# Two local attention steps interleaved on TensorE, Silu in place of Tanh behind the attention, and every mask as a matrix product

## The chip, the cores and the metric

The kernel runs on one core of one Trainium2 chip. The metric is the device time of one execution in microseconds (us). Names of engines in the rows: PE is TensorE's matrix products, PEld its weight loads, DVE is VectorE, ACT is ScalarE, POOL is GpSimd, SP is SyncE, which issues most of the DMAs.

## What is computed

Attention over 4 sequences of 576 tokens with 8 heads of 64, as the sum of a pooled global attention and a banded local one, and behind it two feed-forward layers over all 2304 tokens:

```python
out_d = sm_attn(q_d, k_d, v_d)                 # q, k, v averaged over 4 tokens
out_up = np.repeat(out_d, factor, axis=2)
mask = np.abs(pos[:, None] - pos[None, :]) < factor
scores = scale * np.matmul(q, k.transpose(0, 1, 3, 2))
scores = np.where(mask, scores, -1000000000.0)
attn = np.exp(scores - np.max(scores, axis=-1, keepdims=True))
attn = attn / (np.sum(attn, axis=-1, keepdims=True) + 1e-09)
out_local = np.matmul(attn, v)
x = out_up + out_local                         # then (tokens, 512)

g = x @ w_gate                                 # first layer, width 1536
silu = g * (1.0 / (1.0 + np.exp(-g)))
x = silu * (x @ w_val) @ w_out
h = np.maximum(x @ w_in, 0.0)                  # second layer, width 2048
x = h * h @ w_out2
```

## The kernel before

The whole program is generated by a planner. Work is cut into tasks, each a row of stages; a stage has an engine (`t` TensorE, `v` VectorE, `a` ScalarE, `d` a DMA issued by SyncE, `p` one issued by GpSimd), a planned cost in us, buffers that it takes and gives back, and a condition. `Order.run` keeps a clock for each engine and always issues the stage that can start first, so the order of the instructions on every engine follows from planned costs, due times and buffer counts. The chip then runs these fixed streams with semaphores.

Three kinds of work matter here. **Local steps** (`local_task`): a batch has ten blocks of up to 58 queries against a window of 64 keys, and six steps work on them: steps 0, 1, 3 and 4 on two blocks each, step 2 on one block in each half of the sequence. A step of two blocks makes 16 products `scores` of 64x64 (head pairs `hp`, and `h2` for the two heads of a pair, which lie in rows 0 to 63 and 64 to 127); the softmax over 512 elements a partition; `trans`, four transposes of 128x128; and 16 products `pv`, again 64 rows by 64 columns. In both, `h2` or `r` selects rows `64*r` to `64*r+63` of the operands and the same 64 partitions of the result. All are fp32 products, and each leaves two passes (two rows MATMUL and two LDWEIGHTS) in the records, so a step of two blocks has 32 passes of `scores` and 32 of `pv`. For batches 0 and 1 (`MASK_PE` is 2) the mask is laid into the bank first by bf16 products with an identity; for batches 2 and 3 VectorE multiplies and adds it in `masked`. In the first three steps of batch 0 (`early`) the buffers are borrowed from another pool.

**Global tasks** (`global_tasks`, `global_task`) do the pooled attention with products of 72x144 and 72x72. **Units** (`unit_tasks`) do the first feed-forward layer on 256 tokens: twelve products for the gate and twelve for the value into the banks `gv`, an activation, and twelve products down into `y`. The gate is silu as (tanh(g/2) + 1) * g * v / 2: ScalarE's Tanh (`tanh`), and two VectorE operations (`silu`, `times`). The units of a 256-token tile start once its attention is there, so units and attention alternate on TensorE. Behind the attention a second form of the first layer (`b2_unit`, its `tail` the same gate) and the second layer follow.

Local steps take from shared pools: four PSUM banks `att`, five tiles `p`, two tiles `pt` (transposed probabilities) and two tiles `vw` (the values, loaded by SyncE). Where the planner sees TensorE wait for a bank for more than 0.6 us in the first 100 us, `bank` fills 80% of that wait with products of zeros (line L81); in the first 40 us `warm_bank` does the like (L1251).

Of the kernel before, what the change touches and what calls it, by code (L numbers as in the profile page):

```python
# [1 line left out]

# [61 lines left out]
def attn_moe_kernel(ctx: ExitStack, tc: tile.TileContext, qT, kT, vw, vin, vp, qp, kp, qs, ks, vs, maskc, masks, identc, wB, wC, out):  # L64
# [33 lines left out]
    def dma(size):  # L98
        return size / RATE
# [7 lines left out]
    CUT_T, CUT_J, W_LAG, Q_LATE, Q_LATER, MASK_PE = 2, 4, 65.0, 10.0, 6.0, 2  # L107
# [506 lines left out]
    def local_task(b, i, ins, due, bls=(0, 1), early=False):  # L614
# [11 lines left out]
        nb, b0 = len(bls), bls[0]  # L626
# [8 lines left out]
        def scores():  # L635
            half = int(t00 >= S // 2)
            q, k, o = q_t[b, half], k_t[b, half], HALF0[half]
# [7 lines left out]
            for c, (_, _, q0, w0) in enumerate(blocks):  # L645
                for hp in range(HP):
                    for h2 in range(2):
                        r = slice(64 * h2, 64 * h2 + 64)
                        nc.tensor.matmul(  # L649
                            u["s"][r, c * HP + hp],  # L650
                            q[r, hp, q0 - o : q0 - o + WIN],
                            k[r, hp, w0 - o : w0 - o + WIN],
                            start=not mask_pe,
                            stop=not mask_pe or c * HP + hp == n - 1,
                        )
# [14 lines left out]
        def values():  # L670
            v = room(10, 8 * D) if last else att.tile([128, 8 * D], F32, tag="vw", bufs=N_V, name="vw")
            if b < NB:
                u["v"] = v.rearrange("p (a h l d) -> p l a h d", a=2, h=2, d=D)
                nc.sync.dma_start(out=v, in_=vw[b * NPAIR + i].rearrange("p a h l d -> p (a h l d)"))
                return
            u["v"] = v.rearrange("p (l h a d) -> p l a h d", h=2, a=2, d=D)
            heads = vs[b - NB].rearrange("p f -> (p f)").rearrange("(r h t d) -> r t h d", r=2, h=4, d=D)
            for r in range(2):
                for bl, (_, _, _, w0) in zip(bls, blocks):
                    o = v[64 * r : 64 * r + 64].rearrange("p (l h d) -> p l h d", l=2, d=D)[:, bl]  # L680
                    nc.sync.dma_start(out=o, in_=heads[r, w0 : w0 + WIN])
# [14 lines left out]
        def pv():  # L696
            for t in tiles:
                x_tile(t)
            ps = u["ps"] = bank("att")
            pt = u["pt"].rearrange("p (b a h k) -> p b a h k", b=nb, a=2, h=2)  # L700
            for c, (t0, t1, q0, _) in enumerate(blocks):
                for hpp in range(2):
                    for h2 in range(2):
                        for r in range(2):
                            rr = slice(64 * r, 64 * r + 64)
                            o = (2 * h2 + hpp) * 128 + t0 - t00
                            nc.tensor.matmul(  # L707
                                ps[rr, o : o + t1 - t0],
                                u["v"][rr, bls[c], hpp, h2, :],
                                pt[rr, c, hpp, h2, t0 - q0 : t1 - q0],  # L710
                                start=True,
                                stop=True,
                            )
# [19 lines left out]
        tiles = range(x_of(b * S + t00), x_of(b * S + t11 - 1) + 1)  # L733

        def g_need():
            return [t for c in range(t00 * 2 // S, (t11 - 1) * 2 // S + 1) for t in g_tasks[b, c]]

        def ready():
            when, room = after([v_in] + g_need()), x_room(tiles)
            return None if when is None or room is None else max(when, room)  # L740

        def turn():

            return 0.0 if early or all(t.at > len(t.stages) - 4 for t in g_need()) else None

        v_take = () if last else ("v",)
        v_in = Task([Stage("d", dma(128 * 512) * (1 if b < NB else 2), values, v_take, cond=lambda: task.ready)], due)
        if mask_pe:
            cost, share = 0.737 * nb, 0.74
            softmax = softmax_stages(u, n, 128, WIN, "s", float(D) ** -0.5, 1, False, ("att",))  # L750
        else:
# [1692 lines left out]
```

## Time and profile before

| what | value |
|---|---|
| median of 3 runs | 943.49 us (941.63 to 943.52) |
| the profiled execution | 944.18 us |
| its span, first to last instruction | 942.4 us |
| PE busy | 931.2 us, 99% of the span |
| DVE busy | 757.3 us, 80% |
| ACT busy | 584.5 us, 62% |

A busy PE covers the time in which any product is under way, pipelined ones too, so 99% says that TensorE was hardly ever without work, not that each of its products ran at the array's pace. The chain of waits is followed from end to end: a row of it for several products gives the time by which they moved the end on.

### The profile page before, as it was taken

How to read it: one execution, taken by the hardware profiler on the slowest of the kernel's cores; microseconds unless marked ns; L12 is line 12 of the kernel's file. 1: busy time of each engine (PE TensorE's matmuls, PEld its weight loads, DVE VectorE, ACT ScalarE, POOL GpSimd, SP SyncE). 2: the span in 40 equal slices, each digit the busy share in tenths (PEclk: the TensorE clock that was granted, in tenths of full speed). 3: DMA queues.
4: the chain of work that ended last, by engine and by line, in shares of the span. 5: the costliest groups of instructions: out<-in, count | busy, mean ns of one | idle time of the engine just before them, and what ended most of it. 6: DMA issues, size and time to landing. Idle time of an engine off the chain costs nothing.

```text
span 942.4 us, 22566 instructions
## 1 busy us (share of the span) xinstructions
PE 931.2 (99%) x8929; PEld 907.0 (96%) x8929; DVE 757.3 (80%) x1875; ACT 584.5 (62%) x1368; POOL 23.8 (3%) x31
## 2 busy tenths in 40 slices
PE   8999999999999999999999999999999999999997
PEld 6888999999999999999999999999999999999997
DVE  6998969878978878788796999978777666776865
ACT  3878667657667888456542675757565645555553
POOL 0102102000000000000000000000000000000000
PEclk9999999999999999999999999999999999999999
DMA  9998969586678857166553638624315864516131
GB/s 278 262 286 225 243 186 239 179 270 183 225 269 312 265 172 252 50 220 204 187 185 101 211 138 312 244 81 180 126 77 178 316 230 171 180 67 247 47 133 68
DMA packets 101205, 183.82 MB, mean 195 GB/s; under 512 B 22380, under 2 KB 60012, under 8 KB 101100
## 3 DMA queue, kind: packets, MB, share of 16 engines
q1 hardware_dynamic: 97644, 174.42, 54.8%
q0 software_dynamic: 3456, 7.96, 4.8%
q8 instruction: 70, 1.15, 0.5%
q14 instruction: 35, 0.29, 0.1%
HBM read 120.75 MB, written 61.60 MB: 193 GB/s over the span
## 4 chain that ended last, share of the span: by engine, by line
PE 92%; DVE 2%; ACT 2%; DMA 2%; SPq 1%; issue 0%; DVEq 0%
PE gv L1045 11%; PE gv L1047 10%; PE gv L1046 10%; PE y L1045 8%; PE y L1046 8%; PE y L1047 8%; PE att L1983 6%; PE att L1982 6%; PE att L1981 6%; PE att L1046 3%; PE att L1047 3%; PE att L1045 3%; PE att L707 2%; PE att L797 2%; PE att L649 1%; PE y L1251 1%
## 5 line engine op out<-in xcount | busy, mean ns | idle before, releaser
L1045 PE MATMUL gv<-xs,wg 128*128 128x256 f32 x880 | 250.4, 285 | 0.1
L1046 PE MATMUL gv<-xs,wg 128*128 128x256 f32 x880 | 246.9, 281 | 0.0
L1047 PE MATMUL gv<-xs,wg 128*128 128x256 f32 x880 | 246.9, 281 | 0.0
L1045 PEld LDWEIGHTS gv<-xs,wg 128*128 128x128 f32 x880 | 166.2, 189 | 2.1 <-issue 0.4
L1046 PEld LDWEIGHTS gv<-xs,wg 128*128 128x128 f32 x880 | 166.1, 189 | 0.0
L1047 PEld LDWEIGHTS gv<-xs,wg 128*128 128x128 f32 x880 | 166.0, 189 | 0.0
L2132 ACT ACTIVATE f<-rr 128x256 fp32r<-128x256 f32 (+2 forms) x200 | 88.1, 467 | 62.9 <-PE att L1983 25.7
L1983 PE MATMUL att<-wg,f 128*128 128x256 f32 x432 | 122.5, 284 | 0.5 <-DVE f L2135 0.4
L1982 PE MATMUL att<-wg,f 128*128 128x256 f32 x432 | 122.0, 282 | 0.0
L1981 PE MATMUL att<-wg,f 128*128 128x256 f32 x432 | 121.7, 282 | 0.3 <-ACT f L2132 0.3
L2135 DVE TENSOR_TENSOR f<-rr,f 128x512 fp32r<-128x512 f32 (+2 forms) x200 | 94.0, 488 | 27.2 <-ACT f L2132 26.5
L2056 ACT ACTIVATE rr<-rr 128x512 f32<-128x512 f32 (+1 forms) x144 | 80.2, 557 | 31.4 <-DVE rr L2059 29.2
L1045 PE MATMUL y<-xs,wg 128*128 128x256 f32 x336 | 94.6, 281 | 1.1 <-ACT ys L1228 1.1
L1046 PE MATMUL y<-xs,wg 128*128 128x256 f32 x336 | 94.5, 281 | 0.0
L1047 PE MATMUL y<-xs,wg 128*128 128x256 f32 x336 | 94.4, 281 | 0.0
L1981 PEld LDWEIGHTS att<-wg,f 128*128 128x128 f32 x432 | 81.8, 189 | 0.7 <-ACT f L2132 0.7
L1983 PEld LDWEIGHTS att<-wg,f 128*128 128x128 f32 x432 | 81.2, 188 | 1.4 <-DVE f L2135 1.3
L1982 PEld LDWEIGHTS att<-wg,f 128*128 128x128 f32 x432 | 81.5, 189 | 0.0
L2141 DVE TENSOR_TENSOR rr<-rr 128x256 f32<-128x256 f32 (+1 forms) x160 | 62.3, 393 | 7.0 <-ACT rr L2056 4.7
L1045 PEld LDWEIGHTS y<-xs,wg 128*128 128x128 f32 x336 | 63.6, 189 | 1.4 <-ACT ys L1228 1.3
L1047 PEld LDWEIGHTS y<-xs,wg 128*128 128x128 f32 x336 | 63.5, 189 | 0.0
L1046 PEld LDWEIGHTS y<-xs,wg 128*128 128x128 f32 x336 | 63.5, 189 | 0.1
(149 smaller groups left out, 2317.2 us busy)
## 6 DMA issues: line engine op xcount, KB each, us to landing
wst<-wB SPq DMA_DIRECT2D x36, 512.0 KB, 4.9
w_sp<-tmp SPq DMA_DIRECT2D x36, 512.0 KB, 3.8
wg<-w_sp SPq DMA_DIRECT2D x36, 512.0 KB, 5.1
wst<-wC SPq DMA_DIRECT2D x32, 512.0 KB, 5.0
y_sp<-ys SPq DMA_DIRECT2D x29, 512.0 KB, 4.5
xf_sp<-xs SPq DMA_DIRECT2D x24, 512.0 KB, 2.7
xs<-xf_sp SPq DMA_DIRECT2D x24, 512.0 KB, 5.4
ys<-y_sp SPq DMA_DIRECT2D x20, 512.0 KB, 6.7
```

Of the source, the lines that this page charges most:

```text
L707: nc.tensor.matmul(ps[rr, o : o + t1 - t0], u["v"][rr, bls[c], hpp, h2, :], pt[rr, c, hpp, h2, t0 - q0 : t1 - q0], start=True, stop=True,)
L797: nc.tensor.matmul(us[h2]["s"][:, ci], q, kd_t[b][r, hp, :], start=start, stop=stop)
L1045: nc.tensor.matmul(o, w[:, 0], x[:, 0], start=start, stop=False, skip_group_check=more)
L1046: nc.tensor.matmul(o, w[:, 0], x[:, 1], start=False, stop=False, skip_group_check=more)
L1047: nc.tensor.matmul(o, w[:, 1], x[:, 0], start=False, stop=stop, skip_group_check=more)
L1981: nc.tensor.matmul(o, h, w[:, 0], start=first and not again and c == 0, stop=False, skip_group_check=again)
L1982: nc.tensor.matmul(o, h, w[:, 1], start=False, stop=False, skip_group_check=again)
L1983: nc.tensor.matmul(o, l, w[:, 0], start=False, stop=end, skip_group_check=again)
L2056: return lambda: nc.scalar.activation(out=whole(f, c0), in_=whole(f, c0), func=func)
L2132: nc.scalar.activation(out=fac(k, 0), in_=source(), func=AF.Copy)
L2135: nc.vector.tensor_tensor(out=fac(k, 1), in0=source(), in1=fac(k, 0).bitcast(F32), op=ALU.subtract)
L2141: go = lambda: nc.vector.tensor_tensor(out=o(), in0=a(), in1=b(), op=op)
```

## The change

The stage functions of `local_task` go into `local_lane`, and `local_task` now takes one or two lanes. With two lanes the products of `scores` alternate between them, and so do those of `pv`. Lane 1 exchanges the two halves of the result: products from rows `h2` write partitions of `h2 ^ lane`, into a bank of its own, so that lane 0 uses the two tiles of the array on its diagonal (rows 0, columns 0 and rows 1, columns 1) and lane 1 the two others. Its values are loaded with the halves exchanged. In batch 0 steps 3 and 4 form a pair and the other four stay alone; in batches 1 to 3 the pairs are 0 and 1, the two halves of 2, and 3 and 4. A pair takes two banks `att` for `scores`, two tiles `pt`, both tiles `vw` and two banks for `pv` together; its softmax and transposes stay per lane. `MASK_PE` becomes 4. Units whose activation is planned once all attention is done use ScalarE's Silu and one VectorE product, and `tail` always does.

```diff
-    CUT_T, CUT_J, W_LAG, Q_LATE, Q_LATER, MASK_PE = 2, 4, 65.0, 10.0, 6.0, 2
+    CUT_T, CUT_J, W_LAG, Q_LATE, Q_LATER, MASK_PE = 2, 4, 65.0, 10.0, 6.0, 4
...
+        def score(at):
+            half = int(t00 >= S // 2)
+            q, k, o = q_t[b, half], k_t[b, half], HALF0[half]
+            c, hp = at // HP, at % HP
+            _, _, q0, w0 = blocks[c]
+            for h2 in range(2):
+                nc.tensor.matmul(
+                    u["s"][rows(h2 ^ lane), c * HP + (hp ^ lane)],
+                    q[rows(h2), hp, q0 - o : q0 - o + WIN],
+                    k[rows(h2), hp, w0 - o : w0 - o + WIN],
...
-                nc.sync.dma_start(out=v, in_=vw[b * NPAIR + i].rearrange("p a h l d -> p (a h l d)"))
+                whole = vw[b * NPAIR + i].rearrange("p a h l d -> p (a h l d)")
+                if lane:
+                    for r in range(2):
+                        nc.sync.dma_start(out=v[rows(r)], in_=whole[rows(1 - r)])
+                else:
+                    nc.sync.dma_start(out=v, in_=whole)
...
+        def value(at):
+            pt = u["pt"].rearrange("p (b a h k) -> p b a h k", b=nb, a=2, h=2)
+            c, hpp, h2 = at // 4, at // 2 % 2, at % 2
+            t0, t1, q0, _ = blocks[c]
+            for r in range(2):
+                o = (2 * h2 + hpp) * 128 + t0 - t00
+                nc.tensor.matmul(
+                    u["ps"][rows(r ^ lane), o : o + t1 - t0],
+                    u["v"][rows(r), bls[c], hpp, h2, :],
+                    pt[rows(r), c, hpp, h2 ^ lane, t0 - q0 : t1 - q0],
...
+    def local_task(b, parts, ins, due, early=False):
+
+        lanes = [local_lane(b, i, bls, lane, early) for lane, (i, bls) in enumerate(parts)]
...
+        def scores():
+            for x in lanes:
+                x.masks()
+            for at in range(n):
+                for x in lanes:
+                    x.score(at)
+
+        def pv():
+            for x in lanes:
+                x.begin()
+            for at in range(4 * nb):
+                for x in lanes:
+                    x.value(at)
...
+        cost = 0.63 * nb + nl * 0.107 * nb * (b < MASK_PE)
+        p_take, pt_take, pt_give, v_take = ("p",) * nl, ("pt",), ("pt",) * nl, ("v",)
...
-        halves = ((0, (0, 1)), (1, (0, 1)), (2, (0,))), ((2, (1,)), (3, (0, 1)), (4, (0, 1)))
+        both = (0, 1)
+        ends_ = [(3, both), (4, both)]
+        if b < NB:
+            lanes = [[(0, both)], [(1, both)], [(2, (0,))]], [[(2, (1,))], ends_]
+        else:
+            lanes = [[(0, both), (1, both)]], [[(2, (0,)), (2, (1,))], ends_]
...
         def tanh():
             u["s"] = com.tile([128, T1], F32, tag="sg", bufs=N_SG, name="sg")
+            u["half"] = 0.5 if turned_all() is None else 1.0
+            if u["half"] == 1.0:
+                nc.scalar.activation(out=u["s"], in_=u["g"][:, :n], func=AF.Silu)
+                mid.stages[0].give = mid.stages.pop(1).give
+                return
             nc.scalar.activation(out=u["s"], in_=u["g"][:, :n], func=AF.Tanh, scale=0.5)
...
-            def tanh():
+            def silu():
                 room(t)
-                nc.scalar.activation(out=u[t], in_=gate(), func=AF.Tanh, scale=0.5)
-
-            def silu():
-                nc.vector.scalar_tensor_tensor(out=u[t], in0=u[t], scalar=1.0, in1=gate(), op0=ALU.add, op1=ALU.mult)
+                nc.scalar.activation(out=u[t], in_=gate(), func=AF.Silu)
 
             def times():
-                nc.vector.scalar_tensor_tensor(out=u[t], in0=u[t], scalar=0.5, in1=val(), op0=ALU.mult, op1=ALU.mult)
+                nc.vector.tensor_tensor(out=u[t], in0=u[t], in1=val(), op=ALU.mult)
```

On TensorE, before, the first two local steps of batch 2 stand behind the last products of the global attention (`vd`), one step after the other, each with its own bank:

```order
L1047 MATMUL gv_2416<-xs_1864,wg_1382 128x256
L835 MATMUL att_2445<-pt_2413,vd_1250 64x72 x4
L835 MATMUL att_2452<-pt_2429,vd_1250 64x72 x4
L649 MATMUL att_2462<-kT_1139,qT_1178 64x64 x16
L649 MATMUL att_2490<-kT_1139,qT_1178 64x64 x16
L1045 MATMUL y_2034<-hh_2405,wg_1347 128x256
```

In the changed program the same two steps are one stage, which begins with three mask products (two of 256 columns for the first lane, one of 512 for the second), and the two banks alternate, two products each; the last two rows repeat seven times more:

```order
L881 MATMUL att_2591<-pt_2585,vd_1260 64x72 x4
L649 LDWEIGHTS ident_b_82
L649 MATMUL att_2599<-mask_b_81,ident_b_82 128x256
L649 LDWEIGHTS ident_b_82
L649 MATMUL att_2599<-mask_b_81,ident_b_82 128x256
L649 LDWEIGHTS ident_b_82
L649 MATMUL att_2602<-mask_b_81,ident_b_82 128x512
L657 MATMUL att_2599<-kT_1128,qT_1192 64x64 x2
L657 MATMUL att_2602<-kT_1128,qT_1192 64x64 x2
```

So the sixteen products of bank `att_2602`, which stood behind those of the other bank, now stand between them. Over the whole program the 64x64 products (`scores` and `pv`) lie in 39 unbroken stretches before and in 24 now, mask products go from 16 (12 of 256 columns, 4 of 512) to 32 (24 and 8), and the products of zeros that `bank` puts in from 28 to 49.

On VectorE, behind the attention, a unit's gate before takes L1089 (`silu`) when ScalarE's Tanh is done and L1094 (`times`) when the value is:

```order
L1103 TENSOR_TENSOR hh_5628<-sg_5586,hh_5628 128x256
L379 SCALAR_TENSOR_TENSOR wf_5662<-wst_5434,bits_75 128x512
L1089 SCALAR_TENSOR_TENSOR sg_5660<-sg_5660,gv_5632 128x256
L1366 TENSOR_TENSOR wf_5681<-wf_5606,wf_5662 128x256
L1366 TENSOR_TENSOR wf_5662<-wf_5662 128x256
L1094 SCALAR_TENSOR_TENSOR sg_5660<-sg_5660,gv_5665 128x256
```

After the change only `times` (now L1153) is left of the two:

```order
L1153 SCALAR_TENSOR_TENSOR sg_5319<-sg_5319,gv_5343 128x256
L1418 TENSOR_TENSOR tmp_5358<-wf_5142,tmp_5358 128x512
L1418 TENSOR_TENSOR wg_5363<-wf_5356,wg_5363 128x512
L1162 TENSOR_TENSOR hh_5381<-sg_5319,hh_5381 128x256
L1153 SCALAR_TENSOR_TENSOR sg_5336<-sg_5336,gv_5365 128x256
```

Here the gate's bank is free as soon as ScalarE has read it. That happens in 18 units and in all 54 tails, so 72 VectorE operations leave; ScalarE gains one load of an activation table, ahead of its first Silu.

## Rows read from the trace of the kernel before

**Rows 1.** The page, part 1: busy us (share of the span) xinstructions.

```profile
PE 931.2 (99%) x8929; PEld 907.0 (96%) x8929; DVE 757.3 (80%) x1875; ACT 584.5 (62%) x1368; POOL 23.8 (3%) x31
```

**Rows 2.** Busy time of each engine in stretches (us from the span's start).

```profile
core 0: us, PE busy (x) PEld busy (x) DVE busy (x) ACT busy (x) POOL busy (x), PEclk, DMA share, GB/s
0.00:40.00 40.00, 35.79 (x457) 30.01 (x459) 30.87 (x76) 21.89 (x59) 4.71 (x9) 1.00 0.92 258
40.00:100.00 60.00, 59.76 (x803) 53.16 (x804) 55.62 (x154) 49.10 (x142) 9.52 (x11) 1.00 0.92 264
100.00:270.00 170.00, 169.72 (x2089) 160.51 (x2088) 141.45 (x369) 108.53 (x283) 9.54 (x11) 1.00 0.74 217
270.00:360.00 90.00, 88.92 (x757) 88.62 (x755) 74.59 (x161) 75.61 (x152) 0.00 (x0) 1.00 0.76 255
```

**Rows 3.** Who waited for whom, TensorE: total us, times, longest us.

```profile
PE y L1251 <- ACT zeros L1245: 2.4, 1, 2.4
PE att L649 <- DMA qT<-qT: 1.3, 1, 1.3
PE y L1045 <- ACT ys L1228: 1.1, 1, 1.1
```

**Rows 4.** The chain in order of time, 64x64 stretches: start us, us, what.

```profile
51.04 1.08 PE att L649 x32
...
59.27 1.07 PE att L707 x32
...
185.64 1.54 PE att L707 x48
...
227.60 0.11 PE gv L1047
227.71 2.01 PE att L649 x64
229.72 0.31 PE gv L1045
230.04 0.12 PE gv L1046
```

**Rows 5.** The chain, global attention's products and the transposes.

```profile
57.27 0.59 PE att L686 x4
...
80.33 0.40 PE att L835 x8
...
125.26 1.14 PE att L797 x16
...
140.26 0.64 PE att L797 x8
...
142.76 0.65 PE att L835 x16
```

**Rows 6.** The chain, transposes of two and products of zeros.

```profile
18.97 0.87 PE y L1251 x8
...
54.52 0.37 PE att L686 x2
```

**Rows 7.** Groups by line: busy us, mean ns of one, idle before, releaser.

```profile
L649 PE MATMUL att<-kT,qT 64*64 64x64 f32 x640 | 23.2, 221 | 1.3 <-DMA qT<-qT 1.3
```

**Rows 8.** Groups by line and shape, VectorE and ScalarE.

```profile
L1089 DVE SCALAR_TENSOR_TENSOR sg<-sg,gv 128x256 f32<-128x256 f32 x54 | 22.4, 415 | 6.0 <-ACT sg L1081 5.5
...
L1798 DVE SCALAR_TENSOR_TENSOR ss<-ss,gv 128x256 f32<-128x256 f32 x30 | 12.5, 415 | 8.2 <-ACT ss L1795 8.1
...
L661 DVE SCALAR_TENSOR_TENSOR p<-att,mask 128x256 f32<-128x256 f32 x12 | 4.5, 405 | 0.0
L661 DVE SCALAR_TENSOR_TENSOR p<-att,mask 128x512 f32<-128x512 f32 x4 | 2.7, 674 | 0.0
```

**Rows 9.** Groups of ScalarE in the first 8 us.

```profile
L1245 ACT ACT_TABLE_LOAD x1 | 1.3, 1283 | 0.7 <-PEq L2434 0.7
```

**Rows 10.** The chain: a load of values that landed late.

```profile
95.21 9.48 DMA vw<-vs
```

More of the change, by code (lines that the diff above doesn't have):

```diff
@@ L644, in scores @@
                 nc.tensor.matmul(u["s"][:, c0:c1], ident_b, m, start=c0 == 0, stop=False)
[L645 to L655, printed above, removed]
+        def score(at):
[8 more added lines that the diff above has]
+                    k[rows(h2), hp, w0 - o : w0 - o + WIN],
+                    start=not mask_pe,
+                    stop=not mask_pe or at == n - 1,
+                )
         def masked():
@@ L773, in local_task @@
-        for t in tiles:
-            x_parts[t].append(task)
-        return task
+            if before and not early and not before.done:
+                return None
+            return 0.0 if early or all(t.at > len(t.stages) - 4 for t in g_need) else None
+        cost = 0.63 * nb + nl * 0.107 * nb * (b < MASK_PE)
+        p_take, pt_take, pt_give, v_take = ("p",) * nl, ("pt",), ("pt",) * nl, ("v",)
+        if early:
+            p_take, pt_take = ("xs",) * 3 * lanes[0].first, ()
+            pt_give = ()
+            if lanes[0].last:
+                pt_give = tuple(lambda k=k: ("xs", early_room[k][0]) for k in range(3))
+                v_take = ()
@@ new lines, in local_task @@
+        v_in = [Task([Stage("d", x.load, x.values, v_take, cond=lambda: head.ready)], due) for x in lanes]
+        head = Task([Stage("t", cost, scores, ("att",) * nl + p_take, (), lambda: after(ins + [consts]), 0.7)], due)
+        mids = []
+        for x in lanes:
+            x.softmax[0].cond = lambda: after([head])
+            mids.append(
+                Task(
+                    x.softmax
+                    + [
+                        Stage("t", 0.22 * nb, x.trans, ("att",) + pt_take, () if early else ("p",), turn, 0.98),
+                        Stage("a", act(n * WIN, True), x.turned, (), ("att",)),
+                    ],
+                    due,
+                )
+            )
@@ L777, in global_tasks @@
+        val = Task([Stage("t", 0.64 * nb, pv, ("att",) * nl, pt_give + v_take * nl, ready, 0.7)], due)
+        ends = [Task([Stage("v", dve(232 * nb), x.to_x, (), ("att",), lambda: after([val]))], due) for x in lanes]
+        head.then = [*v_in, *mids, val, *ends]
+        if not early:
+            val_before[0] = val
+        for x, end in zip(lanes, ends):
+            for t in x.tiles:
+                x_parts[t].append(end)
+            att_ends[b].append(end)
+        return head
     def global_tasks(b, ins, due, combos, end=False):
@@ L869, in global_task @@
         return task
-    att_tasks = {}
+    att_tasks, att_heads, att_ends = {}, {}, {b: [] for b in range(B)}
     def x_due(token):
```

93 lines of the change are left out of this document (35 added, 58 removed).

## The prediction, made before the changed kernel ran

> **What bounds the kernel now.** I read the busy times first: TensorE works in 99% of the span, VectorE in 80%, ScalarE in 62% [rows 1]. A high share alone can mislead, so next came who waits. TensorE's waits are few and short: 2.4 us for its first operand, 1.3 us for the first queries, and 1.1 us for ScalarE's copy out of `y` near 358 us [rows 3]. The attention therefore runs at TensorE's pace, and what shortens TensorE's list shortens the kernel, as long as the others keep up. The stretches say where that is tight: from 40 to 100 us VectorE is busy 55.62 of 60 us, from 100 to 270 us 141.45 of 170 [rows 2]. Batch 0 and most of batch 1 fall in the first of these.
>
> **What a local step costs TensorE.** In the chain a stretch of 32 passes of `scores` takes 1.08 us and one of 64 takes 2.01 [rows 4]. The 32 more cost 0.93, so a pass costs 29.1 ns, and 1.08 - 32 x 0.0291 = 0.15 us is paid once for each stretch. For `pv`, 48 passes against 32 give (1.54 - 1.07) / 16 = 29.4 ns. After a stretch the first product of a unit moves the end by 0.31 us where a product usually moves it by 0.12 [rows 4]: up to 0.19 more. A stretch therefore costs 0.15 to 0.34 us beyond its passes.
>
> **Do four tiles run at once?** Before, a 64x64 pass and its partner use the two diagonal tiles, a round of two in 58 ns. No row has four tiles at work, so I bound it by what pairs show. The pace of one tile alone is that of the fp32 transposes: two passes more, of 128 columns each, take 0.59 - 0.37 us [rows 5, 6], 0.11 us a pass or 0.86 ns a column. By it 144 columns take 0.124 us; L797, whose two products lie in different row halves and the same columns, takes (1.14 - 0.64) / 8 = 0.0625 us a pass [rows 5], half of that. And 72 columns take 0.062 us; L835, whose products share rows and lie in different column halves, takes (0.65 - 0.40) / 8 = 0.031 [rows 5], half again. Sharing rows costs nothing and sharing columns costs nothing, so I take it that four passes need the 58 ns of two. That is one end; the other is 117 ns, two rounds. The first is nearer to the rows, since each pair among the four tiles is of a kind that overlaps fully there.
>
> A rule speaks against it. Rows show that the two row halves of `scores` write into one bank in the same round: 640 passes keep TensorE busy for 23.2 us [rows 7], where one after another they would take 640 x 58 ns = 37 us. The Trainium skill, page "TensorEngine Tiling (Array Packing)", section "Restrictions and Gotchas", says that different row tiles cannot access the same PSUM bank simultaneously. By that rule `scores` could not run as it does; if it held, two passes for each bank would follow each other and the gain below would be gone. The measurement decides: it doesn't hold for halves of a bank, and the gain stays.
>
> **The sum, against the profiled execution (944.18 us, 0.7 above the median of the runs).**
>
> 1. Paired passes. Batches 1 to 3 have ten paired blocks each, batch 0 four: 34 blocks x 16 passes = 544 of `scores` and as many of `pv`. 1088 x 29.2 ns = 31.8 us; four at a time they take half: **-15.9 us** (between that and 0). Nothing hides them, since TensorE is the engine that is waited for.
> 2. Stretches. 39 become 24: 15 x 0.25 us, the middle of the two prices above, **-3.8 us** (-2.3 to -5.1).
> 3. Masks. 16 more products, twelve of 256 columns and four of 512, are 20 times 256 columns. Eight products of zeros of that width take 0.87 us [rows 6], 0.109 each: **+2.2 us** on TensorE. VectorE loses the sixteen operations of L661, 4.5 + 2.7 = 7.2 us [rows 8], and then reads its maximum and difference out of PSUM, as it does now for batches 0 and 1.
> 4. Products of zeros. 21 more x 0.109 = **+2.3 us**. They stand for 80% of waits for banks, because a pair takes two of four; the rest of these waits is **+0.6 us**. The low end is 0 for both, if these waits coincide with others.
> 5. VectorE before 100 us. With 4.4 us to spare in 60 [rows 2], it can't follow all of the gain there. Roughly a third of the paired passes fall before 100 us, 5 us of the gain; I take **+1.0 us**, from 0 to 5.
> 6. Silu. 72 VectorE operations of 0.415 us leave [rows 8], 30 us, all behind the attention, where TensorE doesn't wait for VectorE; a gate is ready some 0.4 us sooner. I cost it at **0**: TensorE's other units cover the gate before and after. At most it takes away the 1.1 us wait near 358 us [rows 3]. The table load takes 1.28 us on ScalarE [rows 9], once; queued behind it are that unit's own gate and copies for weights, with units ready on TensorE, and from 270 to 360 us ScalarE has 14 of 90 us to spare [rows 2]. Without that cover it would cost 1.3 us. Silu itself isn't in the trace; I price it as Tanh, which it replaces one for one.
> 7. Values. A pair holds both `vw` tiles, so the next loads wait until its `pv` is done. The slowest load took 9.48 us [rows 10], and between one `pv` and the next the new order has ten us of other products or more. I cost it at **0**, up to 4 us if some land late. What waits behind such a `pv` is all of TensorE's queue. Transposes likewise wait for both `pt` tiles, again behind units that are ready.
>
> Sum: -15.9 - 3.8 + 2.2 + 2.3 + 0.6 + 1.0 = -13.6, so 930.6 us on the profiled execution's own time and some 929.9 against the median. **I predict 930 us.**
>
> **Rivals.**
>
> *TensorE is limited by issue, not by the array.* A `pv` pass has 58 moving columns, a `scores` pass 64, yet both take 29 ns [rows 4]: columns alone don't set the round. If it is the rate at which passes and weight loads are issued, four take twice as long as two, and terms 2 to 5 without the VectorE part remain: 944.18 - 3.8 + 2.2 + 2.3 + 0.6 = 945.5, no change. For it: that equality. Against it: weight loads, which are 64 columns wide in both, explain it as well, and they are per tile. Chance 8%. Halfway between the two ends, a round of 88 ns, half of term 1 is left: 937.5 us, 5%. The Trainium skill, page "TensorE: Matmul & The Clock Gate", section "Wait — 56ns, not 53.3ns?", says that start-to-start never drops below about 25 ns a matmul. No stretch here has a mean below 29, so the trace can't refute it; by that figure a round would take 100 ns and the kernel, an estimate, some 941 us.
>
> *The planned order stalls.* VectorE can't follow before 100 us (5 us of term 5 lost) and some values land late (4 us of term 7): 939 us. For it: VectorE's 93% there, and both `vw` tiles taken. Against: the same engine ran at 93% before and TensorE waited for it nowhere long. 12%.
>
> *Slower: tiles that share rows or columns drain between lanes.* The interleaving puts an off-diagonal pair behind each diagonal one. If each change of pair pays what a stretch pays once, 0.15 us in place of 0.058 [rows 4], 544 changes cost 544 x 0.092 = 50 us, some 995 us; at a fifth of that price 955. It decides as soon as a round of four exceeds 117 ns by 2 or 3. Against it: L797 and L835 overlap partners that share columns or rows. 6% for any price; 2% more for other losses above 16 us.
>
> **How the numbers follow.** My forecast has 67%, stalls 12%, half of the overlap 5%, issue 8%, drain and other losses 8%. Its own range is 926 to 934: the low end takes the higher price of a stretch and no cost for zeros (-1.3 - 2.9), the high end the larger part of the costs of terms 5 and 7. Over all cases 926 to 942 holds about 80%: it reaches over the stalls and the half overlap and leaves out issue and drain. 0.2%, 1.9 us, is about what a measurement of this kernel can tell from no change. Faster by more: 67 + 12 + 5 = 84%; within it, 8% (issue); slower, 8%.
>
> **What would show it.** In the changed kernel's chain a stretch of 64 passes should take about 1.1 us, like 32 now; 2.0 means no overlap, 1.55 half of it. The mask rows of L661 and 72 of VectorE's products should be gone without a change in TensorE's waits; ScalarE should show a second table load after 250 us with no TensorE wait beside it. TensorE waiting for loads of `vw`, for VectorE before 100 us, or for ScalarE near 345 us would show terms 5 to 7 wrong. TensorE's busy sum should fall by some 14 us; if it falls and the span doesn't, the stalls have taken it. The prediction is wrong if four tiles don't overlap.

## The result and the profile after

The changed kernel takes 933.64 us, the median of 4 runs (932.06 to 934.34); the kernel before took 943.5 beside it (941.63 to 943.8). The ratio is 0.9897 with a 95% interval of 0.9879 to 0.9915, so it is faster by 1.0%. The prediction was 930 us with a range of 926 to 942. The profiled execution of the changed kernel took 932.06 us, the fastest of its runs, against 944.18 before: 12.1 us less.

Line numbers have moved: `scores` is L657 now, `pv` L720, the mask products L649, the zeros L82, a unit's three kinds of products L1099 to L1101, the join of a weight tile L380.

The first part of the page answers to [rows 1]: TensorE's busy sum fell by 14.4 us, VectorE's by 28.6.

```profile
PE 916.8 (99%) x8966; PEld 893.5 (96%) x8966; DVE 728.7 (78%) x1787; ACT 585.7 (63%) x1369; POOL 23.7 (3%) x31
```

The stretches of [rows 2] again. From 40 to 100 us TensorE is no longer always busy; from 270 to 360 us VectorE has 7.4 us less to do.

```profile
40.00:100.00 60.00, 58.33 (x884) 52.13 (x881) 55.04 (x153) 47.27 (x137) 9.10 (x11) 1.00 0.99 275
...
270.00:360.00 90.00, 88.73 (x748) 88.04 (x746) 67.20 (x143) 72.13 (x144) 0.00 (x0) 1.00 0.73 242
```

Who waited for whom on TensorE, as in [rows 3]. The first and third rows have their like before. New are waits for VectorE and ScalarE at L1100 and L1099 (both for `h`, the squared gate of a `b2_unit`), and one at L720 for "issue", that is, for nothing that the profile shows. No row names `vw`.

```profile
PE y L1310 <- ACT zeros L1304: 2.4, 1, 2.4
PE att L1100 <- DVE h L1864: 1.2, 1, 1.2
PE y L1099 <- ACT ys L1287: 1.2, 1, 1.2
PE att L720 <- issue: 1.0, 1, 1.0
PE att L1099 <- ACT h L1861: 0.8, 1, 0.8
```

The chain in order of time (start, us, what). A stretch of 64 passes takes 1.09 us, where [rows 4] have 2.01. At 98.69 the one wait for issue stands, behind 127 passes in a row; at 235.82 another 64 of `pv` follow 64 of `scores` directly, without a wait.

```profile
96.68 1.09 PE att L657 x64
97.77 0.92 PE att L720 x63
98.69 1.00 issue
99.70 0.21 PE att L720
...
234.73 1.09 PE att L657 x64
235.82 0.94 PE att L720 x64
```

The groups of [rows 7] and [rows 9]: the passes of `scores` keep TensorE busy for 14.1 us, 23.2 before, and a second table load stands with the first Silu.

```profile
L657 PE MATMUL att<-kT,qT 64*64 64x64 f32 x640 | 14.1, 222 | 0.7 <-DMA qT<-qT 0.7
```

```profile
L1137 ACT ACT_TABLE_LOAD x1 | 1.3, 1283 | 0.0
```

**Where the time came from and went.** I divided TensorE's list at three places and took from each part what its unit products need at the pace they keep wherever nothing disturbs them, 0.118 us from start to start. The attention's part is the start of the last `pv` pass less 0.118 for each unit product ahead of it. The rest of a part is what it loses: behind the attention up to the first product of a `b2_unit` into `y`; from there to the first product of the second layer (the `b2_unit`s); and from there to the last product. All the kernels of this study are in the table, with their median and, as a measure of how far weights are, the number of weight tiles joined (L379 before, L380 after) when TensorE starts its 2050th unit product, early in the `b2_unit`s.

```
kernel                median   attention  lost up   lost in      lost in       weight tiles at
                      us       us         to b2     b2_units     layer 2       product 2050
before                943.5    127.3      0.9       1.2          6.8           50
after                 933.64   112.6      1.1       4.7          5.8           47
e1_lanes_apart        942.85   123.4      0.5       4.7          5.7           47
e2_tanh               938.53   113.0      1.7       9.1          6.7           46
e3_masks_vector       937.30   112.5      2.9       9.2          5.7           46
e4_no_zeros           931.71   115.0      2.1       1.2          5.7           48
e5_before_silu        943.16   127.0      2.7       0.3          5.7           50
e6_before_masks       948.57   130.7      3.7       1.7          6.7           49
e7_dues_19_5          935.98   112.7      3.3       4.0          5.8           47
e9_pairs_alone        939.54   112.4     -0.1      12.4          6.8           45
e10_low_on_gpsimd     940.71   117.9      0.6       9.5          5.7           47
e11_first_3           936.97   113.9      3.1       2.6          9.9           48 (four fewer wanted)
e12_before_first_3    965.15   126.9      2.6       9.3         18.6           48 (four fewer wanted)
e14_no_zeros_early    938.78   117.7      6.1       0.4          5.8           49
```

From before to after the attention gave 14.8 us and the second layer 1.0; the `b2_unit`s took 3.5 back, and 0.1 went behind the attention: 12.1 us. The 3.5 are the loss that no term of the prediction held. Of them 2.7 are TensorE's starts at 368.94 and 376.21 to 376.67, which come 1.41, 0.94 and 0.34 us later than the pace. The wait for `ys` is a matter of where it is counted: its start at 346.69 us, 1.35 late, falls into the `b2_unit`s, and its like before, at 359.15 and 1.25 late, into the column ahead of them. In that column of the changed kernel stand two new late starts instead, by 0.42 us at 268.97 and by 0.31 at 272.49.

The chain there, of the changed kernel: the sums and the gate of a `b2_unit`, whose steps stand between other work on VectorE and ScalarE.

```profile
365.84 0.42 DVE ss L1804
366.33 0.20 issue
366.52 0.40 DVE ss L1857
366.93 0.54 issue
367.46 0.42 DVE ss L1804
367.94 0.18 issue
368.13 0.42 DVE ss L1804
368.55 0.34 DVE h L1864
368.94 0.38 PE att L1100
```

### The profile page after: what moved, and what is told of

It reads as the page before. It is cut to its first block, busy times and chain, and to the rows that moved or that the text cites. A ratio compares the mean times of both kernels' runs of the same rounds, so it can differ in the third digit from the quotient of the medians.

```text
span 930.3 us, 22554 instructions
## 1 busy us (share of the span) xinstructions
PE 916.8 (99%) x8966; PEld 893.5 (96%) x8966; DVE 728.7 (78%) x1787; ACT 585.7 (63%) x1369; POOL 23.7 (3%) x31
## 4 chain that ended last, share of the span: by engine, by line
PE 95%; DVE 2%; ACT 1%; DMA 1%; issue 1%; SPq 0%; DVEq 0%; ACTq 0%
PE gv L1099 11%; PE gv L1101 11%; PE gv L1100 11%; PE y L1099 9%; PE y L1100 8%; PE y L1101 8%; PE att L2038 6%; PE att L2037 6%; PE att L2036 6%; PE att L1100 3%; PE att L1101 3%; PE att L1099 3%; PE att L843 2%; PE att L657 1%; PE att L881 1%; PE att L720 1%
## 5 line engine op out<-in xcount | busy, mean ns | idle before, releaser
L1099 PE MATMUL gv<-xs,wg 128*128 128x256 f32 x880 | 250.4, 285 | 0.3 <-ACT sg L1137 0.3
L1101 PE MATMUL gv<-xs,wg 128*128 128x256 f32 x880 | 246.9, 281 | 0.1
L1100 PE MATMUL gv<-xs,wg 128*128 128x256 f32 x880 | 246.9, 281 | 0.0
L1099 PEld LDWEIGHTS gv<-xs,wg 128*128 128x128 f32 x880 | 166.1, 189 | 2.8 <-issue 1.0
L1101 PEld LDWEIGHTS gv<-xs,wg 128*128 128x128 f32 x880 | 165.9, 189 | 0.3 <-DVE wg L427 0.3
L1100 PEld LDWEIGHTS gv<-xs,wg 128*128 128x128 f32 x880 | 166.0, 189 | 0.0
L1100 PE MATMUL y<-xs,wg 128*128 128x256 f32 x336 | 94.5, 281 | 0.0
L1099 PE MATMUL y<-xs,wg 128*128 128x256 f32 x336 | 94.5, 281 | 0.0
L1101 PE MATMUL y<-xs,wg 128*128 128x256 f32 x336 | 94.4, 281 | 0.0
L1099 PEld LDWEIGHTS y<-xs,wg 128*128 128x128 f32 x336 | 63.5, 189 | 0.2 <-ACT ys L1287 0.2
L1100 PEld LDWEIGHTS y<-xs,wg 128*128 128x128 f32 x336 | 63.5, 189 | 0.1
L1101 PEld LDWEIGHTS y<-xs,wg 128*128 128x128 f32 x336 | 63.6, 189 | 0.0
```

The costliest lines, as they stand in the source:

```text
L1099: nc.tensor.matmul(o, w[:, 0], x[:, 0], start=start, stop=False, skip_group_check=more)
L1100: nc.tensor.matmul(o, w[:, 0], x[:, 1], start=False, stop=False, skip_group_check=more)
L1101: nc.tensor.matmul(o, w[:, 1], x[:, 0], start=False, stop=stop, skip_group_check=more)
```

## The theory and its rivals

Weights reach the chip packed. A tile `wst` costs ScalarE two or three passes (L368, L377, for most also L373) and VectorE the join (L380); then each half of a product's operand is made, one operation on ScalarE (L1414) and one on VectorE (L1418), and for the later weights VectorE forms sums of tiles too (L1425). The queue of weights is worked off beside the attention and the units, in one order, and the `b2_unit`s need weights that come after four groups which only the second layer wants. My theory: the shorter attention takes from ScalarE and VectorE the time in which they unpacked. Product 2050 starts at 370.7 us before and at 357.3 after; from the attention's end to the first `b2_unit` the kernel before joined 18 tiles in 90.2 us, 5 us a tile, so 13.4 us less is 2.7 tiles, and 47 are done in place of 50. This is an estimate of what the planner could place, and the agreement is rough: when the attention ends 31 tiles are joined, 30 before, so all three are lost behind it, and VectorE is not full there (busy for 69.3 of the 93.1 us up to product 2050, 85.6 of 101.7 before). The rows of VectorE's join from the start to that product, of the kernel before and of the changed one:

```profile
L379 DVE SCALAR_TENSOR_TENSOR wf<-wst,bits 128x512 int32<-128x512 int32 x50 | 34.2, 685 | 3.0 <-ACT wst L376 2.5
```

```profile
L380 DVE SCALAR_TENSOR_TENSOR wf<-wst,bits 128x512 int32<-128x512 int32 x47 | 32.3, 688 | 4.6 <-ACT wst L377 3.1 <-DMA wst<-wB 1.1
```

On this theory Silu and the masks are not side issues: both take work from VectorE just where its part of the unpacking is late. The rivals: the waits come from Silu itself (its planned gate is shorter, its table load late); from the attention's late end among the units (673 unit products lie between the last `pv` and the first `b2_unit`, 757 before); or from the order of the gate's own steps. And for the gain: it comes from fewer stretches and another order, not from four tiles at once.

In the expectations that follow, "the second layer's first units" are the `b2_unit`s, and "the third layer" is the second layer proper.

## The experiments

An edit also makes the planner order the engines anew. Only with the lanes apart do VectorE and ScalarE keep the order of the changed kernel. In every other variant the order of TensorE's products changes too from some point on, so such a run shows an edit together with its new order.

**Lanes one after the other.** All passes of lane 0 are issued ahead of those of lane 1; the rest is the changed kernel.

```diff
-            for at in range(n):
-                for x in lanes:
+            for x in lanes:
+                for at in range(n):
                     x.score(at)
...
-            for at in range(4 * nb):
-                for x in lanes:
+            for x in lanes:
+                for at in range(4 * nb):
                     x.value(at)
```

> Edit: in a paired step all passes of lane 0 are issued, then all of lane 1, in scores and in pv; the count of passes, stretches and masks stays, and a round uses two tiles again. If the gain comes from four tiles at work at once (1088 paired passes, 14.6 ns less for each), the time rises by 15.9 us to about 949.5, and a stretch of 64 passes takes about 2.0 us in place of 1.09. If the gain comes from fewer stretches and another order, the time stays at 933.6 and a stretch of 64 passes stays near 1.1. If TensorE's reordering lets neighbouring passes of the two lanes overlap at the seam only, less than 1 us of 15.9 is kept.

It took 942.85 us (ratio to before 0.9999, 0.9990 to 1.0008): the whole gain is gone, but 9.2 us came back, not 15.9. Its chain says why:

```profile
48.54 1.84 PE att L657 x62
66.31 1.83 PE att L720 x63
...
118.45 0.89 PE att L720 x31
```

A stretch of 64 takes 1.84 us, not 2.01. In the starts the last passes of lane 0 and the first of lane 1 pair up at the seam, and the stretch from its first start to its last is 1.69 us, 1.86 before and 0.94 with lanes interleaved. Twenty such seams keep 20 x 0.17 = 3.4 us of the gain. Fourteen stretches of 64 and six of 32 lose 14 x 0.75 + 6 x 0.28 = 12.2 us, and the late start at 99.70 us (by 1.1) doesn't appear: 11.1, against 123.4 - 112.6 = 10.8 in the attention's column. The last-named expectation of under 1 us at the seams was too low. The overlap of four tiles is what makes the changed kernel faster: 10.8 of the 14.8 us that the attention gave are lost without it, and by this account 3.4 more are overlap that stays at the seams.

The `b2_unit`s lose 4.7 us here as they do without this edit, with the same late starts (1.41, 0.94 and 0.34 us), and 47 tiles are joined at product 2050 again, though that product starts at 367.5 us in place of 357.2. This limits the theory. The attention takes 10.8 us longer on the chip, but VectorE and ScalarE use hardly any of it: up to its end they are busy for 226.3 and 183.9 us here, and for 224.5 and 183.4 in the changed kernel. The lanes apart first, then the changed kernel (columns as in [rows 2]):

```profile
0.00:274.90 274.90, 270.91 (x3456) 250.76 (x3458) 226.30 (x591) 183.89 (x492) 23.70 (x31) 1.00 0.80 231
```

```profile
0.00:264.10 264.10, 259.07 (x3458) 238.67 (x3458) 224.46 (x590) 183.42 (x492) 23.72 (x31) 1.00 0.83 240
```

So the tiles are missing in the planned order, and more time on the chip doesn't bring them back. Where the theory speaks of time that the attention takes from unpacking, it can only be time in the plan.

**Tanh again.** The changed kernel with `tanh`, `silu` and `times` of the kernel before, in `b2_unit`s and in the units behind the attention.

```diff
-            u["half"] = 0.5 if turned_all() is None else 1.0
+            u["half"] = 0.5
...
-                nc.scalar.activation(out=u[t], in_=gate(), func=AF.Silu)
+                nc.scalar.activation(out=u[t], in_=gate(), func=AF.Tanh, scale=0.5)
```

> Edit: Tanh and the two VectorE products return for the gate; everything else is as in the changed kernel. If Silu costs and gives nothing (term 6 at 0), the time stays at 933.6 within 1 us, with 30 us more of VectorE and no second table load. If Silu's shorter planned gate or its table load causes the new waits near 268, 369 and 376 us (0.5 + 1.5 + 0.5 us), the time falls to about 931 and these waits are gone. If VectorE's lighter load behind the attention was a gain, the time rises by 1 us or more.

938.53 us, 0.9954 (0.9940 to 0.9968): 4.9 us slower than with Silu. The waits near 369 and 376 grew, so Silu doesn't cause them; the third expectation holds. The wait at 269 behind the table load is gone, as it had to be. From 264 to 357 us VectorE makes 18 products that the changed kernel hasn't:

```profile
L1148 DVE SCALAR_TENSOR_TENSOR sg<-sg,gv 128x256 f32<-128x256 f32 x18 | 7.5, 418 | 3.7 <-ACT sg L1140 3.5
```

The chain of this kernel ahead of a late `b2_unit` runs through the unpacking itself, ScalarE's L368, L373 and L377, VectorE's L380 and ScalarE's L1414 in turn, with hardly any gap:

```profile
368.21 0.61 DVE wf L380
368.85 0.63 ACT wg L424
369.48 0.52 ACT wg L1414
370.00 0.69 ACT bits L368
370.70 0.63 ACT bits L373
371.33 0.25 ACT wh L1414
371.58 0.58 ACT wst L377
372.19 0.70 DVE wf L380
```

**Masks of batches 2 and 3 on VectorE again**, in the changed kernel.

```diff
-    CUT_T, CUT_J, W_LAG, Q_LATE, Q_LATER, MASK_PE = 2, 4, 65.0, 10.0, 6.0, 4
+    CUT_T, CUT_J, W_LAG, Q_LATE, Q_LATER, MASK_PE = 2, 4, 65.0, 10.0, 6.0, 2
```

> Edit: batches 2 and 3 add their mask on VectorE again (16 operations of L661), 20 times 256 columns of products leave TensorE. If TensorE is the bound there and VectorE has room, the time falls by 2.2 us to 931.4. If VectorE, with pairs that need their softmax at once, needs the 7 us itself, the time stays or rises by up to 3 us.

937.30 us, 0.9943 (0.9930 to 0.9955): 3.7 us slower. The attention's part didn't move (112.5), although 16 products left TensorE. VectorE's operations are back, 7.3 us of them, most in one shape:

```profile
L669 DVE SCALAR_TENSOR_TENSOR p<-att,mask 128x256 f32<-128x256 f32 x12 | 4.6, 408 | 0.1
```

The attention ends earlier among the units, at 257.0 us in place of 264.1, with 28 weight tiles joined in place of 31. At product 2050 it is 46 in place of 47, and the `b2_unit`s lose 9.2 us.

**No products of zeros in waits for banks.**

```diff
-    PAD_END, PAD_WAIT, PAD_SHARE = 100.0, 0.6, 0.8
+    PAD_END, PAD_WAIT, PAD_SHARE = 0.0, 0.6, 0.8
```

> Edit: no products of zeros in free time of TensorE's plan (49 in the changed kernel, 5.3 us of starts). If they were paid for on top of the waits (terms 4 at its upper end), the time falls by 2.3 us or more, to 931 or less. If they only fill waits for banks and for VectorE that would be there without them, the time stays at 933.6 and TensorE shows some 5 us more of waits before 100 us. If the granted clock falls from 2.4 to 1.2 GHz in a stretch without them, the time rises.

931.71 us, 0.9883 (0.9869 to 0.9896), against the changed kernel's 0.9897 (0.9879 to 0.9915) no difference that these runs can tell. The attention's part rose by 2.4 us: waits took the place of the zeros, and the granted clock fell to 0.50, the lower level, from 62 to 68 us behind a wait of 2.7 us:

```profile
62.00:64.00 2.00, 1.76 (x6) 1.47 (x7) 1.97 (x6) 2.00 (x8) 0.00 (x0) 0.50 1.07 389
...
66.00:68.00 2.00, 2.00 (x59) 1.89 (x52) 1.97 (x6) 0.57 (x2) 0.00 (x0) 0.50 1.07 389
```

In exchange the `b2_unit`s lose 1.2 us only, with 48 weight tiles in place of 47 in this order. Both ends of the expectation were right about a part, and together they cancel.

**Silu alone and the masks alone, on the kernel before.** The first is that part of the change's diff; the second the constant.

```diff
-            def tanh():
-                room(t)
-                nc.scalar.activation(out=u[t], in_=gate(), func=AF.Tanh, scale=0.5)
-
             def silu():
-                nc.vector.scalar_tensor_tensor(out=u[t], in0=u[t], scalar=1.0, in1=gate(), op0=ALU.add, op1=ALU.mult)
+                room(t)
+                nc.scalar.activation(out=u[t], in_=gate(), func=AF.Silu)
```

> Edit: the kernel before, with Silu in place of Tanh and its first VectorE product behind the attention, nothing else. Theory: Silu's 30 us of VectorE count only where the second layer's first units wait for unpacked weights, and that wait came with the shorter attention; the kernel before has none there (its one wait near 359 us is 1.4 us), so the time stays at 943 or falls by at most 1.4. Rival: Silu is worth the 4.9 us by which Tanh slowed the changed kernel wherever it stands: 938.

943.16 us, 0.9996 (0.9988 to 1.0005): no change in the total. In its parts 0.9 us less is lost in the `b2_unit`s and 1.0 less in the second layer, but 1.8 more behind the attention, where a start at 278.46 us comes 1.0 late behind VectorE's part of a gate. Silu is worth nothing to the kernel before and 4.9 us to the changed one.

```diff
-    CUT_T, CUT_J, W_LAG, Q_LATE, Q_LATER, MASK_PE = 2, 4, 65.0, 10.0, 6.0, 2
+    CUT_T, CUT_J, W_LAG, Q_LATE, Q_LATER, MASK_PE = 2, 4, 65.0, 10.0, 6.0, 4
```

> Edit: the kernel before, with the masks of batches 2 and 3 as products on TensorE, nothing else. Theory: as above, VectorE's 7 us there hide nothing in the kernel before, and 20 times 256 columns come on top: +2.2, some 945. Rival: the relief of VectorE is worth the 3.7 us that the masks on VectorE cost the changed kernel: 939.

948.57 us, 1.0060 (1.0047 to 1.0073): slower by 4.8 us, twice what the products account for. In its profiled execution the attention's part is 3.4 us longer, and 2.8 more are new waits behind it, near 279 and from 362 to 367 us, in another order of the units. So the masks too turn their sign: +4.8 here, -3.7 in the changed kernel.

**Only the pairing left**: the edits of the second and the third experiment together.

> Edit: the changed kernel with Tanh and with the masks of batches 2 and 3 on VectorE: of the change only the pairing is left. If VectorE's and ScalarE's time is what lacks behind a shorter attention, both reliefs missing cost at least what each alone cost (Tanh +4.9, masks on VectorE +3.7): 938 to 943, with waits for weights from 340 to 390 us. If the two costs were accidents of one order each, they needn't add, and 931 (the sum of the prediction without masks) to 938 is what comes.

939.54 us, 0.9961 (0.9949 to 0.9974). The attention's part is 112.4, the shortest of all, and the `b2_unit`s lose 12.4 us, the most of all, with 45 weight tiles. Pairing gives 14.9 us and keeps 4. Silu alone on top of it (the masks' experiment) is worth 2.2 us by the medians, the masks alone (the Tanh experiment) 1.0, which the intervals hardly tell from nothing, both 5.9: more than their sum.

**Attention earlier among the units.**

```diff
-    W_DUE0, W_STEP, X_DUE0, X_STEP, X_STEP0 = 17.0, 2.2, 12.0, 20.0, 14.0
+    W_DUE0, W_STEP, X_DUE0, X_STEP, X_STEP0 = 17.0, 2.2, 12.0, 19.5, 14.0
```

> Edit: the changed kernel with the constant that spaces the due times of attention's tiles from 20 to 19.5 us, so that the plan puts attention earlier among the same units (744 products of units between the last pv and the first unit of the second layer, 672 before the edit). If the new waits near 369 and 376 us come from attention's late end among the units, so that fewer weights are unpacked behind it, they go and the time falls by some 3 us to 930 or 931. If what lacks is ScalarE's and VectorE's time before that point, 13 us of which went with the shorter attention, the waits stay, moved or grown, and the time is 933 or more.

935.98 us, 0.9924 (0.9911 to 0.9937), not faster. The waits stand at 370.6 and 377.9, nearly as long as in the changed kernel, with 47 tiles at product 2050, although 72 more unit products lie behind the attention. That speaks against the attention's late end as their cause.

**A part of VectorE's work on GpSimd.** The low halves of streamed weights are subtracted there, planned at 1.28 us each.

```diff
-                nc.vector.tensor_tensor(
+                e = nc.gpsimd if stream else nc.vector
+                e.tensor_tensor(
                     out=w[:, 1, :n], in0=u["f", f].bitcast(F32)[:, :n], in1=w[:, 0, :n].bitcast(F32), op=ALU.subtract
                 )
```

> Edit: the changed kernel with the subtraction that makes the low half of a streamed weight (VectorE, 0.69 us each, spilled to memory and not needed soon) on GpSimd. If VectorE's time before the second layer is what lacks, the waits near 369 and 376 us shrink and the time falls by 2 to 3.5 us, to 930 to 931.5. If ScalarE's three passes for each weight set the pace, or GpSimd is too slow and holds the buffers, the time stays or rises.

940.71 us, 0.9964 (0.9952 to 0.9977): slower by 7.1. GpSimd takes 1.25 us for what VectorE does in 0.62:

```profile
L1419 POOL TENSOR_TENSOR tmp<-wf,tmp 128x512 fp32r<-128x512 f32 (+1 forms) x52 | 64.8, 1250 | 263.8 <-ACT tmp L1414 238.5 <-DVE ss L1805 9.4 <-DMA wst<-wC 7.4
```

No weight came earlier: 47 tiles at product 2050, and 49 at product 2150, where the changed kernel has 51. The attention's part grew by 5 us too. Whether `wf` buffers held longer or ScalarE set the pace, the run doesn't tell; it was the wrong relief.

**Three groups ahead instead of four.** Four weight tiles of the second layer move behind those of the `b2_unit`s. TensorE's products stay the same, but their order doesn't, though the expectation says so: the planner puts them in another order from 339 us on.

```diff
-N_FIRST, N_DIRECT, N_PUT = 4, 2, 1
+N_FIRST, N_DIRECT, N_PUT = 3, 2, 1
```

> Edit: the changed kernel with three instead of four groups of later weights unpacked ahead of the second layer's first weights, so four weight tiles (12 passes of ScalarE, some 25 operations of VectorE) move behind that point; TensorE's list is the same. If ScalarE's and VectorE's time before the second layer is what lacks, the waits near 369 and 376 us go, the count of weights unpacked by then no longer matters, and the time falls by 2.5 to 3.5 us to 930 or 931. If these waits come from the order of the gate's own steps (Silu, product, two halves) and not from weights, they stay, and so does 933.6. If the moved group is late for the third layer, the time rises.

The waits near 369 and 376 us are gone. The busy time of the engines from 365 to 390 us, of the changed kernel first, then of this one (PE, PEld, DVE, ACT):

```profile
365.00:390.00 25.00, 22.94 (x190) 22.34 (x189) 19.95 (x47) 18.48 (x40) 0.00 (x0) 1.00 0.45 149
```

```profile
365.00:390.00 25.00, 25.00 (x215) 25.00 (x214) 14.45 (x36) 11.17 (x27) 0.00 (x0) 1.00 0.13 42
```

This is the strongest sign that these waits come from unpacking that only the second layer needs. It doesn't settle it, since the order is new as well and part of the loss only moves: from 344 to 350 us four starts come 2.7 us late in sum, where the changed kernel has one by 1.35. The time is 936.97 us, 0.9932 (0.9919 to 0.9946), slower than the changed kernel. The moved group is late: TensorE waits at the start of the second layer, which loses 9.9 us in place of 5.8. The attention costs 1.3 us more and the stretch behind it 2.0, together more than the 2.1 won in the `b2_unit`s.

```profile
PE att L2036 <- ACT f L2187: 2.6, 3, 1.3
```

> Edit: the kernel before with three groups ahead instead of four, as in the edit of the changed kernel. If the lack of ScalarE's and VectorE's time came with the shorter attention, the kernel before gains nothing from it: 943 within 1 us. If it gains 2.5 us too, the relief is not what the change made scarce.

The same edit makes the kernel before slower by 22 us: 965.15, 1.0234 (1.0219 to 1.0248), lost mostly from 572 to 609 us. Neither expectation held. It has no wait near 370 to win; why it loses so much more than the changed kernel is not shown (Tanh, which leaves VectorE less room, is a guess).

**Without zeros, and the second layer's weights due from 110 us on.**

```diff
-    PAD_END, PAD_WAIT, PAD_SHARE = 100.0, 0.6, 0.8
+    PAD_END, PAD_WAIT, PAD_SHARE = 0.0, 0.6, 0.8
...
-    S_DUE, S_STEP = 140.0, 15.0
+    S_DUE, S_STEP = 110.0, 15.0
```

> Edit: the changed kernel without products of zeros in waits for banks, and the later weights due from 110 us on in place of 140. In the order of VectorE 29 weight tiles stand ahead of the last softmax step, 27 without the earlier dues and in the changed kernel. If weights unpacked by the second layer's start decide, there is no wait from 360 to 385 us, and the time is that without zeros (931.7) or up to 1.5 us less, below both kernels. If the earlier weights take VectorE from attention, TensorE's waits before 270 us grow, and the time is 932 to 936.

938.78 us, 0.9950 (0.9937 to 0.9962). The `b2_unit`s lose 0.4 us, with 49 tiles: that part came true. But the weights took their time from the attention (117.7) and from the units behind it, where one start comes 2.4 us late at 270.44. By these parts the same engines pay either way. No version of the study is shown to beat the changed kernel.

## Why the prediction was right, and where it was off

The total came within the range, 3.7 us above the 929.9 of the sum. Of these 1.5 lie in the terms (930.6 was summed for the profiled execution, 932.06 came), and the other 2.2 in where the two profiled executions lie among their runs: 0.7 above the median before, 1.6 below it after. That the terms miss by so little is in part luck: the attention came 1.2 us better than they say and the second layer 1.0, which they leave out, against 3.5 us lost in the `b2_unit`s.

1. *Paired passes, -15.9.* Right. From the first start to the last, 64 paired passes take 0.943 us and 32 take 0.478: 14.5 ns a pass, 29.2 before. The lanes one after the other show the source. The row halves of `scores` in one bank still run together, and now four tiles do. The rule of the Trainium skill that was weighed there (page "TensorEngine Tiling (Array Packing)", section "Restrictions and Gotchas") doesn't hold for halves of a bank in these runs. Nor does the floor of about 25 ns from start to start that the Trainium skill gives (page "TensorE: Matmul & The Clock Gate", section "Wait — 56ns, not 53.3ns?"): 14.5 is the mean here. The kernel before could have refuted that floor already, against what the prediction says: the two passes of a pair start 6 or 7 ns apart there, and only the mean is 29.
2. *Stretches, -3.8*, and 3., *masks on TensorE, +2.2.* Not measured one by one. Terms 1 to 5 made -13.6 and the attention's part fell by 14.8. The starts of the mask products did grow by 2.4 us (3.4 to 5.8). But the price of term 3 was only half of the matter: taking these products out again didn't shorten the attention, and putting back VectorE's 7 us, which the prediction let go for nothing, made the kernel 3.7 us slower.
4. *Zeros, +2.3 and +0.6.* At its low end. The starts of the zeros did grow by 2.3 us (3.0 to 5.3), but without any of them the attention takes longer: they stand in waits that exist.
5. *VectorE before 100 us, +1.0.* It is there: the chain of the changed kernel runs through VectorE from 58.65 to 62.72 us while 29 products of zeros fill the time on TensorE. Its price alone wasn't measured.
6. *Silu, 0.* **This is the step that failed**: "TensorE's other units cover the gate before and after." In the kernel before the total bears this out (Silu alone: 0.9996, no change). In the changed one they don't cover it: a gate stands between unpacking on ScalarE and VectorE and comes late, and 30 us less of VectorE are worth 4.9 us. The table load, priced at 0 under cover, is on the chain at 267.24 us and makes one start 0.4 us late; with the attention earlier among the units a start there, at 261.68, is 1.5 us late.
7. *Values, 0.* Right: TensorE waits for no `vw`.

What the sum had no term for is the 3.5 us lost in the `b2_unit`s. I read [rows 2] from 270 to 360 us (VectorE 74.59 and ScalarE 75.61 of 90) as room, and asked for each edit who covers it; I didn't ask what those engines were doing there, by when it had to be done, and how much of their time the shorter attention would take in the plan. That missing tiles are the cause is the reading that fits best, since tiles and loss go together over the variants: with 50, 49 or 48 tiles at product 2050 the `b2_unit`s lose 0.3 to 1.7 us, with 47 tiles 4.0 to 4.7 (9.5 with GpSimd), with 46 or 45 tiles 9.1 to 12.4, the two variants with three groups left aside. No run changes the number of tiles and leaves the order of the products as it is, so it is argued, not shown. The "planned order stalls" rival came nearest in kind, but placed the stalls before 100 us and at the values.

Of the rivals, issue, half the overlap and a drain between lanes are refuted by the 1.09 us stretch. What stays open is the wait for issue near 99 us, 1.0 us in the changed kernel and up to 1.8 in its variants. It stands there wherever 64 interleaved passes of `scores` and 64 of `pv` follow each other directly, and not with the lanes apart, nor without zeros, where products of a unit lie between; but at 235 us the same sequence has no wait. One packet of the DMA queue that the profile names "instruction" falls between 96 and 101 us; that it is the cause is only a guess.

## What to carry to other kernels

When the engine that bounds a kernel gets a stage done sooner, the engines beside it can lose time for their background work: count what they must have finished by the next deadline, not just their busy share. Where a planner fixes the order of every engine, look for this in the plan: a stage that runs longer on the chip than planned gave nothing back here. An edit that is free while there is cover (here Silu) can be worth much after another edit has removed it, and one that costs (here the masks) can turn into a gain, so parts of a change are to be priced together, in the state in which the others leave the kernel. Products that use different tiles of the array are worth interleaving, since even passes that only meet at a seam overlap.

## What was not expected of the hardware

Passes of different tiles overlap across the seam of two runs of their own kind, for some 0.17 us each time. And a wait of TensorE can cost more than its length: in the kernel with Tanh a start came 2.4 us late at 379.3 us, and behind it the granted clock lay near its lower level for 4 us. The columns of the windows as in [rows 2]; the last but two is the granted clock:

```profile
377.50:380.00 2.50, 0.38 (x1) 0.19 (x1) 2.50 (x8) 2.50 (x6) 0.00 (x0) 1.00 0.54 187
380.00:382.00 2.00, 1.92 (x9) 1.93 (x10) 1.97 (x5) 0.35 (x1) 0.00 (x0) 0.54 0.57 186
382.00:384.00 2.00, 2.00 (x13) 2.00 (x13) 1.05 (x3) 0.94 (x2) 0.00 (x0) 0.60 0.92 320
384.00:386.00 2.00, 2.00 (x19) 2.00 (x19) 0.42 (x1) 0.00 (x0) 0.00 (x0) 1.00 0.08 27
```

By these rows 2 x 0.46 + 2 x 0.40 = 1.7 us were lost to the clock there. In the kernel with pairs alone a start as late, at 371.13 us, had no such sequel: the granted clock stayed at 1.00.
